# Retention and a rational feed-forward on one core: VectorE's order in the first steps of the feed-forward

## The chip, the cores and the metric

The kernel runs on one core of one Trainium2 chip. The metric is the device time of an execution in microseconds. TensorE (PE) multiplies, VectorE (DVE), ScalarE (ACT) and GpSimd (POOL) work element by element, SyncE's queue (SP) issues the transfers between HBM and the on-chip memory SBUF. Matmuls write into PSUM, a second on-chip memory that VectorE and ScalarE can read and write and GpSimd cannot.

## The reference

```python
B, H, S, D = 8, 8, 576, 64             # q, k, v: [B, H, S, D]
scores = (q @ k.T) / sqrt(D)           # per batch and head
ret = scores * gamma[h] ** (i - j)     # for i >= j, else 0; gamma[h] = 1 - 2 ** (-5 - h)
x = (ret @ v) -> [B * S, H * D]        # 4608 tokens x 512
h = x @ w_in                           # 512 -> 2048
P = a0 + a1 h + a2 h^2 + a3 h^3
Q = 1 + |b0| |h| + |b1| h^2
out = (P / (Q + 1e-6)) @ w_out         # 2048 -> 512
```

All inputs and outputs are 32-bit floats.

## The kernel before, in words

**Retention.** The tokens are cut into 36 units of 128. For a unit n, `scale_q` (GpSimd) and `scale_v` (ScalarE, eight instructions on the tile kv) scale its q and v by powers of gamma; `scores` multiplies k and q on TensorE; `decay` clears two corners of the tile s (GpSimd) and masks the scores into the rest (three VectorE instructions from PSUM). `outputs` multiplies the masked scores with v, the keys with v for the running state, and the old state with q, all into one PSUM tile ps. `add` and `fade` update the state S_sb (VectorE, then GpSimd). `keep_hi` (ScalarE) rounds the outputs to xhi, and `keep_lo` (VectorE) keeps the rest as xlo.

**Feed-forward.** The tokens are nine blocks of 512, the hidden width sixteen strips f of 128. One step works on one block and one strip (b, f). Each product is formed from high and low parts in three passes: `gemm1` is twelve matmuls into h, `gemm2` twelve into acc, three or four steps later. In between stands the rational function, spread over three steps:

- in the step of the block itself: `ffn_p` (p = a3 h + a2 and u = |h| on ScalarE, p = p h on VectorE), `ffn_p2` (VectorE, p = (p + a1) h), `ffn_va` (ScalarE, v from u), `ffn_v` (VectorE, v = v u);
- in the next: `ffn_r` (ScalarE, u = 1/Q by a logarithm and an exponential), `ffn_q` (VectorE, the quotient and one Newton factor, two instructions), `ffn_q3` (VectorE, their product);
- in the one after: `ffn_hi` (ScalarE, g high) and `ffn_lo` (g low, on GpSimd in the first 24 blocks).

h and ps lie in PSUM. u, v, p and g are in SBUF, with one exception: in steps 8 to 21 u lies in a free bank of PSUM, the tile `free_at`.

**Weights.** They arrive as raw 64-bit words (bits) and are brought into two parts in the course of the first steps: `start` (ScalarE, tile c), `split0` (VectorE, a shift of c), `split1` and `split2` (VectorE, integer operations on c and bits), `split3` (ScalarE's high part of w, then GpSimd's low part). A weight is started in one step, where `split0` follows at the end, and goes through `split1` to `split3` in the next. `STARTS` says how many are started in each step: one or two in steps 0 to 4, one in each later step.

**Order.** Each engine executes its instructions in the order in which the program writes them, and that order is written out by hand: a list of names for a step, of which `run` calls those that have something to do. So one list sets the order of VectorE, ScalarE, GpSimd, TensorE and SP at once. `BEFORE` holds for the stage ahead of the first step; `FIRST` where u is in SBUF and the step is below 24, that is in steps 0 to 7 and in 22 and 23; `MID` in steps 8 to 21; `DENSE`, `REST` and `END` after that.

```python
SCORES = [1, 3, 5, 23, 25, 27, 29, *range(2 * NF, (NB - 1) * NF, 4)]
...
        run(END if not this else MID if free_at else FIRST if i < first else DENSE if i < 2 * NF else REST, todo)
        load_weights(2)
```

In steps 1, 3, 5 and 23 a unit's scores are formed and masked; its outputs, sum, fade and x parts follow in the next step, in which the q and v of the unit after it are scaled too. Step 0 has the outputs of unit 4. Loads are issued by SP: a unit's two loads when the outputs of the unit two before it are written into the program, two weights at the end of a step as long as there are any.

Of the kernel before, what the change touches and what calls it, by code (L numbers as in the profile page):

```python
# [31 lines left out]

BEFORE = "split1 start scale_q scale_v scores decay outputs split2 add fade keep_hi keep_lo split3 split0".split()
FIRST = (
    "split1 gemm1 outputs ffn_p split2 ffn_hi keep_hi ffn_lo gemm2 ffn_r scale_q split3 add fade keep_lo start ffn_p2"
    " scale_v scores decay split0 ffn_q ffn_q3 ffn_va ffn_v"
).split()
MID = (
    "split1 split2 gemm1 ffn_p ffn_r ffn_hi ffn_lo split3 ffn_va gemm2 ffn_p2 ffn_q ffn_v ffn_q3 start split0"
# [532 lines left out]
```

## Time and profile before

| | |
|---|---|
| median of 3 runs | 962.99 us (962.88 to 964.47) |
| the profiled execution | 965.23 us, its span from first to last instruction 963.4 us |
| mean granted TensorE clock | 0.981 |
| busy: TensorE, VectorE, ScalarE, GpSimd | 922.9, 830.7, 708.9, 164.4 us |

In a row of a timeline stand the start in us from the span's start, the duration in us, the engine, the source line (L66 is the helper through which every instruction passes, so tiles tell them apart), the operation, the tiles out<-in, the sizes, and the number of equal instructions that the row merges. Brackets give idle time of the engine just ahead of the row and what ended it. An instruction's row overlaps the next one's by some 0.08 us, so the time that an instruction takes in a sequence is the distance of two starts. In the table of stages each row is a stretch of the span, with the busy time of each engine in it, the granted clock, the share of the DMA engines and their rate.

Step 0 begins at about 37 us, step 8 at about 110, step 22 at about 193 and step 24 at about 209, by VectorE's rows.

### The profile page before, as it was taken

The numbers are of one execution on the slowest core, as the hardware profiler recorded it, in microseconds if no ns is written. First come the engines' busy times: TensorE is split into PE (matmuls) and PEld (weight loads), VectorE is DVE, ScalarE is ACT, GpSimd is POOL, SyncE is SP. The second block draws the span as 40 slices with busy tenths as digits, with TensorE's granted clock in tenths as the row PEclk, the third lists the DMA queues.
The fourth block names the chain that finished last, engine by engine and source line by source line (L and its number), as shares of the span: only waits on it lengthen the run. The fifth ranks groups of instructions, "written<-read, shape, count | busy, mean of one in ns | idle before, by whom it ended". The sixth has DMA issues, their size and how long they took to land.

```text
span 963.4 us, 16126 instructions
## 1 busy us (share of the span) xinstructions
PE 922.9 (96%) x6234; PEld 750.2 (78%) x6234; DVE 830.7 (86%) x1261; ACT 708.9 (74%) x1274; POOL 164.4 (17%) x200
## 2 busy tenths in 40 slices
PE   7678889999999999999999999999999999999997
PEld 6556768877888888888888888888888888888886
DVE  3899999997889888888888888888888888888895
ACT  5477788876767778777777777777877777767775
POOL 4445444451201111010001111101111111100000
PEclk9789999999999999999999999999999999999999
DMA  9944100012221111210021112110211121001001
GB/s 347 407 183 181 39 0 1 1 45 89 88 80 53 45 45 52 80 45 25 30 80 44 44 45 88 44 67 22 88 45 45 45 88 45 1 1 45 1 0 45
DMA packets 20557, 65.44 MB, mean 68 GB/s; under 512 B 2304, under 2 KB 2432, under 8 KB 20480
## 3 DMA queue, kind: packets, MB, share of 16 engines
q1 hardware_dynamic: 20480, 64.41, 18.5%
q8 instruction: 49, 0.80, 0.4%
q14 instruction: 28, 0.23, 0.1%
HBM read 54.96 MB, written 9.44 MB: 67 GB/s over the span
## 4 chain that ended last, share of the span: by engine, by line
PE 79%; DVE 8%; ACT 6%; DMA 5%; issue 1%; POOL 1%; SPq 0%; ACTq 0%; POOLq 0%
PE acc L66 36%; PE h L66 34%; PE ps L66 8%; DMA bits<-in_w_in 3%; DVE p L66 3%; DVE c L66 2%; ACT free_at L66 2%; DVE v L66 2%; DMA bits<-in_w_out 1%; ACT v L66 1%; ACT w L66 1%; DMA qk<-in_qkv 1%; ACT g L66 1%; ACT o L66 0%; DVE s L66 0%
## 5 line engine op out<-in xcount | busy, mean ns | idle before, releaser
L66 PE MATMUL acc<-w,g 128*128 128x512 f32 x1632 | 403.7, 397 | 5.4 <-ACT o L66 5.4
L66 PE MATMUL h<-xhi,w 128*128 128x512 f32 x1152 | 381.5, 392 | 5.2 <-DVE p L66 2.7
L66 PEld LDWEIGHTS acc<-w,g 128*128 128x128 f32 x1632 | 304.9, 190 | 75.1 <-ACT o L66 6.3
L66 PEld LDWEIGHTS h<-xhi,w 128*128 128x128 f32 x1152 | 217.7, 189 | 52.6 <-DVE p L66 3.9
L66 PE MATMUL h<-xlo,w 128*128 128x512 f32 x576 | 225.6, 392 | 0.0
L66 ACT ACTIVATE p<-h,ab_sb 128x512 f32<-128x512 f32 x144 | 111.6, 775 | 108.2 <-PE h L66 108.1
L66 PEld LDWEIGHTS h<-xlo,w 128*128 128x128 f32 x576 | 108.8, 189 | 22.7 <-DVE xlo L66 0.4
L66 DVE TENSOR_TENSOR p<-p,h 128x512 f32<-128x512 f32 x144 | 98.8, 686 | 26.8 <-ACT u L66 26.3
L66 ACT ACTIVATE u<-h 128x512 f32<-128x512 f32 x130 | 77.5, 596 | 59.9 <-DVE v L66 58.3
L66 DVE SCALAR_TENSOR_TENSOR p<-p,ab_sb,u 128x512 f32<-128x512 f32 x130 | 97.8, 753 | 25.7 <-ACT u L66 22.5
L66 DVE TENSOR_TENSOR v<-v,u 128x512 f32<-128x512 f32 x130 | 91.1, 701 | 28.5 <-ACT v L66 28.4
L66 DVE SCALAR_TENSOR_TENSOR p<-p,ab_sb,h 128x512 f32<-128x512 f32 x144 | 107.2, 744 | 3.6
L66 ACT ACTIVATE v<-u,absb 128x512 f32<-128x512 f32 x130 | 104.7, 806 | 1.2 <-DVE p L66 0.9
L66 DVE SCALAR_TENSOR_TENSOR p<-v,p 128x512 f32<-128x512 f32 x144 | 100.5, 698 | 4.5
L66 ACT ACTIVATE u<-u,lnb 128x512 f32<-128x512 f32 x130 | 94.2, 724 | 4.2
L66 ACT ACTIVATE u<-v,lnb 128x512 f32<-128x512 f32 x130 | 92.8, 714 | 2.0 <-DVE v L66 2.0
L66 DVE TENSOR_TENSOR g<-p,g 128x512 fp32r<-128x512 f32 x112 | 91.4, 816 | 1.4 <-ACT g L66 1.4
L66 ACT ACTIVATE g<-p 128x512 fp32r<-128x512 f32 x136 | 85.5, 629 | 8.8 <-DVE p L66 4.2
L66 DVE SCALAR_TENSOR_TENSOR v<-v,u 128x512 f32<-128x512 f32 x130 | 90.7, 698 | 0.0
L66 POOL TENSOR_TENSOR S_sb<-S_sb,gv_sb 128x256 f32<-128x256 f32 x32 | 20.4, 637 | 403.5 <-DVE S_sb L66 401.4
L66 ACT ACTIVATE kv<-kv,gv_sb 128x64 f32<-128x64 f32 x288 | 72.6, 339 | 11.1 <-DMA kv<-in_qkv 5.6
L66 DVE TENSOR_TENSOR s<-ps,mask_sb 64x256 f32<-64x256 f32 (+1 forms) x108 | 55.0, 509 | 11.7 <-PE ps L66 10.7
(43 smaller groups left out, 696.5 us busy)
## 6 DMA issues: line engine op xcount, KB each, us to landing
qk<-in_qkv SPq DMA_DIRECT2D x36, 512.0 KB, 4.9
kv<-in_qkv SPq DMA_DIRECT2D x36, 512.0 KB, 4.0
bits<-in_w_in SPq DMA_DIRECT2D x16, 512.0 KB, 10.2
bits<-in_w_out SPq DMA_DIRECT2D x16, 512.0 KB, 10.2
out<-o SPq DMA_DIRECT2D x16, 512.0 KB, 3.5
out<-o SPq DMA_DIRECT2D x4, 256.0 KB, 2.4
gq_sb<-in_gq SPq DMA_DIRECT2D x1, 256.0 KB, 2.7
mask_sb<-in_masks SPq DMA_DIRECT2D x1, 160.0 KB, 5.1
```

Source lines behind the costliest of these rows:

```text
L66: return lambda *a, **k: self.tc.keep_in_program_order(method(*a, **k))
```

## The change

One list is rewritten. It contains the same names.

```diff
 FIRST = (
-    "split1 gemm1 outputs ffn_p split2 ffn_hi keep_hi ffn_lo gemm2 ffn_r scale_q split3 add fade keep_lo start ffn_p2"
-    " scale_v scores decay split0 ffn_q ffn_q3 ffn_va ffn_v"
+    "split1 split2 gemm1 outputs ffn_p ffn_r ffn_hi ffn_lo keep_hi split3 ffn_va gemm2 ffn_p2 add fade keep_lo"
+    " ffn_q ffn_v ffn_q3 start scale_q scale_v scores decay split0"
 ).split()
 MID = (
     "split1 split2 gemm1 ffn_p ffn_r ffn_hi ffn_lo split3 ffn_va gemm2 ffn_p2 ffn_q ffn_v ffn_q3 start split0"
```

What each engine executes in a step, in order (names stand for the instructions that the engine has of them):

| engine | before | after |
|---|---|---|
| VectorE | split1, ffn_p, split2, add, keep_lo, ffn_p2, decay, split0, ffn_q, ffn_q3, ffn_v | split1, split2, ffn_p, ffn_p2, add, keep_lo, ffn_q, ffn_v, ffn_q3, decay, split0 |
| ScalarE | ffn_p, ffn_hi, keep_hi, ffn_r, split3, start, scale_v, ffn_va | ffn_p, ffn_r, ffn_hi, keep_hi, split3, ffn_va, start, scale_v |
| GpSimd | ffn_lo, scale_q, split3, fade, decay | ffn_lo, split3, fade, scale_q, decay |
| TensorE | gemm1, outputs, gemm2, scores | the same |

## The prediction

> **What bounds the kernel now.** I read the page's busy times first, then the table of stages, then each engine's timeline in the stages that the change touches.
>
> ```profile
> PE 922.9 (96%) x6234; PEld 750.2 (78%) x6234; DVE 830.7 (86%) x1261; ACT 708.9 (74%) x1274; POOL 164.4 (17%) x200
> ```
>
> ```profile
> core 0: us, PE busy (x) PEld busy (x) DVE busy (x) ACT busy (x) POOL busy (x), PEclk, DMA share, GB/s
> 73.80:92.50 18.70, 16.20 (x128) 13.02 (x128) 18.02 (x27) 13.60 (x27) 9.80 (x9) 0.91 0.59 226
> 140.00:185.00 45.00, 45.00 (x200) 37.28 (x199) 43.82 (x71) 39.24 (x65) 19.53 (x16) 1.00 0.00 1
> 200.00:215.00 15.00, 12.88 (x95) 9.90 (x85) 14.94 (x22) 11.16 (x25) 6.53 (x7) 0.89 0.21 71
> ```
>
> Over the whole span TensorE is the bound. The table shows where it is not: in 73.8 to 92.5 (steps 4 and 5) VectorE is busy for 18.02 of 18.70 us and TensorE only 16.20; in 200 to 215 (the end of step 22, steps 23 and 24) it is 14.94 against 12.88 of 15. From 140 to 185 (the middle order) TensorE has no idle time at all. So a microsecond that VectorE gains or loses in the early steps moves the start of a stretch that TensorE fills, and reaches the end nearly whole.
>
> VectorE in steps 4 and 5, in the order of before (start, duration):
>
> ```profile
> 76.52 0.68 DVE L66 SCALAR_TENSOR_TENSOR c<-bits,c 128x512 int32<-128x512 int32 x1
> 77.12 0.68 DVE L66 TENSOR_TENSOR p<-p,h 128x512 f32<-128x512 f32 x1
> 77.72 1.17 DVE L66 SCALAR_TENSOR_TENSOR c<-bits,c 128x512 int32<-128x512 int32 x1
> 78.81 0.41 DVE L66 TENSOR_TENSOR S_sb<-S_sb,ps 128x256 f32<-128x256 f32 x1
> 79.15 0.68 DVE L66 TENSOR_TENSOR xlo<-ps,xhi 128x512 fp32r<-128x512 f32 x1
> 79.75 0.73 DVE L66 SCALAR_TENSOR_TENSOR p<-p,ab_sb,h 128x512 f32<-128x512 f32 x1
> 81.06 1.83 DVE L66 TENSOR_SCALAR c<-c 128x512 int32<-128x512 int32 x2 [0.58 <-ACT c L66]
> 82.81 0.74 DVE L66 SCALAR_TENSOR_TENSOR p<-p,ab_sb,u 128x512 f32<-128x512 f32 x1
> 84.79 0.69 DVE L66 TENSOR_TENSOR v<-v,u 128x512 f32<-128x512 f32 x1
> 85.40 2.38 DVE L66 SCALAR_TENSOR_TENSOR c<-bits,c 128x512 int32<-128x512 int32 x2
> 88.30 1.28 DVE L66 SCALAR_TENSOR_TENSOR c<-bits,c 128x512 int32<-128x512 int32 x2
> 90.17 1.55 DVE L66 TENSOR_TENSOR s<-ps,mask_sb 128x512 f32<-128x512 f32 x3
> 91.64 1.12 DVE L66 TENSOR_SCALAR c<-c 128x512 int32<-128x512 int32 x1
> 95.26 0.68 DVE L66 SCALAR_TENSOR_TENSOR c<-bits,c 128x512 int32<-128x512 int32 x1
> 116.91 0.41 DVE L66 TENSOR_SCALAR c<-c 128x512 int32<-128x512 int32 x1
> ```
>
> The two steps last from 76.52 to 95.26, 18.74 us. Equal instructions take unequal times: an integer operation 0.68 or 1.17, two of them 1.28 or 2.38, the shift 0.41 (116.91) or 1.12. GpSimd's rows of the same time, and a close-up of one meeting, say why:
>
> ```profile
> 76.80 1.55 POOL L66 TENSOR_TENSOR g<-p,g 128x512 fp32r<-128x512 f32 x1 [2.53 <-issue]
> 78.30 1.74 POOL L66 TENSOR_TENSOR qk<-qk,gq_sb 128x512 f32<-128x512 f32 x1
> 80.55 1.30 POOL L66 TENSOR_TENSOR w<-c,w 128x512 fp32r<-128x512 f32 x1 [0.51 <-ACT w L66]
> 81.81 0.79 POOL L66 TENSOR_TENSOR S_sb<-S_sb,gv_sb 128x256 f32<-128x256 f32 x1
> 85.95 1.28 POOL L66 TENSOR_TENSOR g<-p,g 128x512 fp32r<-128x512 f32 x1 [3.35 <-ACT g L66]
> 89.73 2.51 POOL L66 TENSOR_TENSOR w<-c,w 128x512 fp32r<-128x512 f32 x2 [2.49 <-ACT w L66]
> ```
>
> ```profile
> 112.26 1.28 POOL L66 TENSOR_TENSOR g<-p,g 128x512 fp32r<-128x512 f32 x1 [4.99 <-ACT g L66]
> 113.50 1.74 POOL L66 TENSOR_TENSOR w<-c,w 128x512 fp32r<-128x512 f32 x1
> 112.77 1.31 DVE L66 SCALAR_TENSOR_TENSOR p<-p,ab_sb,u 128x512 f32<-128x512 f32 x1
> 114.01 1.77 DVE L66 SCALAR_TENSOR_TENSOR v<-v,u 128x512 f32<-128x512 f32 x1
> 119.09 1.27 POOL L66 TENSOR_TENSOR g<-p,g 128x512 fp32r<-128x512 f32 x1 [3.85 <-issue]
> 120.18 0.75 DVE L66 SCALAR_TENSOR_TENSOR p<-p,ab_sb,free_at 128x512 f32<-128x512 f32 x1
> ```
>
> At 112.77 VectorE's quotient operation, all in SBUF, starts while GpSimd subtracts; it ends at 114.08, 0.54 after GpSimd's end at 113.54. GpSimd's next subtraction then takes 1.74 instead of 1.28, and VectorE's next operation 1.77 instead of 0.68: the two take turns. At 120.18 the same operation meets the same subtraction with its u in PSUM (free_at) and takes 0.75. Likewise the mask (90.17, from PSUM) takes its 1.55 beside two GpSimd subtractions. So **an SBUF-only VectorE operation that meets a GpSimd tensor operation loses up to 1.1 us (1.77 − 0.68); one on PSUM loses nothing**. Page SBUF — State Buffer of the Trainium skill, section Who interferes with whom, gives the rule: a VectorE instruction with two SBUF inputs contends with a GpSimd one that reads SBUF, whole instruction against whole instruction. The rows agree. That rule speaks against this change, which puts SBUF operations side by side.
>
> **The old pair of steps.** Collisions: 1.17 − 0.68 = 0.49 at 77.72; 1.83 − 2 x 0.41 = 1.0 at 81.06; 2.38 − 1.28 = 1.10 at 85.40; 1.12 − 0.41 = 0.71 at 91.64. Together 3.3. Waiting for ScalarE: 0.58 (81.06). The work itself is 18.74 − 3.3 − 0.58 = 14.86.
>
> **The change part by part.** No instruction and no DMA is added or removed; the list reorders VectorE, ScalarE and GpSimd. TensorE's and SP's own orders stay, so SP's loads stay in line behind the same outputs and only follow them in time; the units and weights that are loaded then are used many steps later, and I cost that at nothing. It holds in steps 0 to 7, and also in 22 and 23, which use the same list.
>
> *VectorE.* A step is now: integer operations; p x h, second p product, then (even steps) state sum and x's low part, all from PSUM; quotient, quotient, v, last product, all SBUF; (odd steps) the mask; the shifts. The PSUM run is 2 x 0.6 + 0.34 + 0.6, some 2.2 us, in an even step (start-to-start times of the rows 77.12, 78.81, 79.15 and 79.75) and 1.3 in an odd one. The SBUF run is 85.40 − 82.81 = 2.6.
>
> *GpSimd.* Scaling q goes from before the weight's subtraction to behind the state's fade. What releases its operations in an even step? ScalarE's x high part, which waits for TensorE's outputs, stands in front of ScalarE's weight copy; the fade waits for VectorE's sum; scaling q waits behind both. In the old order g and q (76.80 to 80.04) lay beside one integer operation and three PSUM operations, and cost 0.49. In the new order weight, fade and q all become ready when the PSUM run ends, and take turns with the SBUF run: 1.1 + 0.4 + 1.1 = 2.6 (the fade's 0.79 is shorter by 0.5, and loses half of itself, my choice between 0 and 0.79). The block's own g subtraction follows ScalarE's logarithm and exponential, which now stand early in its step; it meets the shift or an integer operation: 1.1, between 0 and 1.1. In an odd step g meets the third integer operation, 1.1, and of two weight subtractions one meets the quotient, 1.1 (0.6 to 2.2). Sum 5.9, bounds 3 to 7.
>
> *The mask and TensorE's outputs.*
>
> ```profile
> 73.79 2.29 PE L66 MATMUL ps<-s,kv 128*64 128x128 f32 x15 [4.59 <-POOL s L66]
> 77.83 3.02 PE L66 MATMUL acc<-w,g 128*128 128x512 f32 x12
> ```
>
> TensorE already idles 4.59 us for the masked scores (GpSimd's zeros come with them); the outputs then take 73.79 to 77.83, 4.0 us, at a low clock. In the old order VectorE has the shift, the SBUF run, two integer operations and p x h between mask and state sum: 0.4 + 2.6 + 1.2 + 0.6 = 4.8 us of work, enough for the 4.0. In the new order only the shift, two integer operations and two PSUM products lie between: 0.4 + 1.2 + 1.3 = 2.9 without collisions, 4.0 with the one of g above. So VectorE waits for outputs by 0 to 1.5; I take 0.4. The old 0.58 wait for ScalarE's integer preparation goes, since the shift stands last.
>
> New pair: 14.86 + 5.9 + 0.4 = 21.2 against 18.74, **+2.5 for steps 4 and 5** (bounds −0.5 to +4).
>
> *Other early steps.* Steps 2 and 3 are the same, but the first g there falls on PSUM work (TensorE is late with its block), one collision less: +1.4. Steps 6 and 7 have no q to scale (the next scores are in step 23): 2.5 − 1.1 = +1.4. In steps 0 and 1 q of unit 5 now waits behind two weight subtractions and the fade (2.51 + 0.79, rows 89.73 and 81.81), and the scores on TensorE wait with it; TensorE waits for that unit's mask anyway. One collision there goes, two come: +0.5. Sum for steps 0 to 7: 0.5 + 1.4 + 2.5 + 1.4 = **+5.8**.
>
> *Steps 22 and 23.*
>
> ```profile
> 201.91 1.19 DVE L66 SCALAR_TENSOR_TENSOR c<-bits,c 128x512 int32<-128x512 int32 x1
> 203.68 1.55 DVE L66 TENSOR_TENSOR s<-ps,mask_sb 128x512 f32<-128x512 f32 x3
> 205.48 1.54 PE L66 MATMUL ps<-s,kv 128*64 128x128 f32 x16 [2.08 <-POOL s L66]
> ```
>
> TensorE idles 2.08 here for the mask. The mask now stands behind the SBUF run of 2.6, in which the weight's subtraction and the next unit's q scaling meet it (1.1 for one of them), and the collision of the integer operation at 201.91 goes (1.19 − 0.68 = 0.5): **+3.2** on TensorE (bounds +1 to +4.5), which is full again behind it.
>
> **Sum.** 5.8 + 3.2 = 9.0. The profiled execution took 965.23 with a span of 963.4; the median of the runs is 962.99, 2.2 lower. 965.2 + 9.0 = 974.2 for such an execution, 963.0 + 9.0 = 972.0 for the median.
>
> A second page bears on it: TensorE: Matmul & The Clock Gate, part The HAM clock gate, says that about 3.4 us without matmuls halve TensorE's clock until as long a busy stretch has passed. The rows agree: sixteen matmuls at 205.48, behind 2.08 us, take 1.54, fifteen at 73.79, behind 4.59, take 2.29. By it the longer gap at 205 makes the outputs there slow as well: that is the last rival.
>
> **The rivals.**
> *Faster: the PSUM run covers GpSimd.* If the weight, fade and q operations end before the SBUF run starts, the pair falls to 14.86 + 0.5 for waits, 3.4 less than now; over steps 2 to 7 about 8 less, against +2.6 for the later mask in step 23: 963 − 5.5, about 957.5. It decides at whether outputs end 3 us before VectorE's low part. For it: GpSimd is busy only 9.80 of 18.70. Against: the mask's new place makes the outputs end when the PSUM run does. 13%.
> *No change, within 0.2% (1.9 us, about what a measurement of this kernel can tell from none).* Collisions only change place, 3.3 for 3.3, and the step-23 mask is hidden by the 2.08 that TensorE waits anyway: 963. Against: that wait ends with the mask itself. 6%.
> *Half of it.* Only the mask's delay in step 23 counts, or only steps 0 to 7: 963 + 3 to 5.8, 966 to 969. 18%.
> *More: TensorE's clock.* If the idle time before the outputs of steps 6 and 24 grows past what 73.79 shows, both take 4.0 instead of some 2.7 (4.0 x 1.54 / 2.29), and VectorE and ScalarE wait for them in turn: 2 x 1.3 and as much again, 3 to 6 more, 975 to 978. 15%.
> My forecast, 969 to 975: 48%.
>
> **How the numbers follow.** Faster 13%, same 6%, slower 48 + 18 + 15 = 81%. Predicted is the forecast's 972.0. The range 963 to 977.5 leaves out the faster case and the top of the last rival, under 2 in 10.
>
> **What would show it.** Right: in the new timeline the quotients and v of even steps show 1.2 to 1.8 beside weight, fade and q on GpSimd, which take turns; the pair of steps 4 and 5 takes over 20 us; TensorE's idle time for the masked scores grows in steps 2, 4, 6 and at the start of step 24 (2.08 to about 5); the stage of the middle order is as before but starts 5 to 6 us later. Wrong: the SBUF run stays at 2.6 in even steps, GpSimd's weight and q rows lie beside p x h and the low part, or TensorE's gaps shrink.

## The result, and the profile after

The changed kernel takes 974.46 us (973.88 to 974.76, 4 runs) against 963.68 (962.88 to 964.47, 4 runs): the ratio is 1.0107, with a 95% interval of 1.0093 to 1.0122. By that ratio it is slower by 10.3 us, 9.0 to 11.8. One of the ten executions of the run mixed below took 4127.63 us and is not in its ratio. The profiled execution took 974.76, its span 972.9 against 963.4.

The page's busy times, and the table of stages (steps 4 and 5 now last from 77.7 to 99.2):

```profile
PE 923.7 (95%) x6234; PEld 751.3 (77%) x6234; DVE 836.2 (86%) x1261; ACT 708.0 (73%) x1274; POOL 165.9 (17%) x200
```

```profile
77.70:99.20 21.50, 17.11 (x130) 13.86 (x131) 20.48 (x28) 13.51 (x27) 10.68 (x10) 0.82 0.42 148
150.00:195.00 45.00, 45.00 (x201) 37.24 (x200) 42.45 (x69) 38.48 (x64) 20.46 (x16) 1.00 0.00 1
210.00:225.00 15.00, 9.19 (x59) 7.19 (x59) 11.26 (x16) 5.88 (x11) 6.19 (x6) 0.77 0.22 71
```

VectorE's busy time grew by 5.5 us with the same 1261 instructions (830.7 before). The middle order is as full of TensorE work as before. In the stretch around step 24 TensorE is busy for only 9.19 of 15.00 us.

VectorE in steps 4 and 5, then GpSimd in the same time:

```profile
77.74 2.37 DVE L66 SCALAR_TENSOR_TENSOR c<-bits,c 128x512 int32<-128x512 int32 x2
82.30 0.42 DVE L66 TENSOR_TENSOR S_sb<-S_sb,ps 128x256 f32<-128x256 f32 x1 [0.82 <-ACT xhi L66]
83.24 1.47 DVE L66 SCALAR_TENSOR_TENSOR p<-p,ab_sb,u 128x512 f32<-128x512 f32 x1
84.64 1.10 DVE L66 SCALAR_TENSOR_TENSOR v<-v,u 128x512 f32<-128x512 f32 x1
85.66 1.78 DVE L66 TENSOR_TENSOR v<-v,u 128x512 f32<-128x512 f32 x1
92.42 0.93 DVE L66 SCALAR_TENSOR_TENSOR p<-p,ab_sb,u 128x512 f32<-128x512 f32 x1
93.27 1.78 DVE L66 SCALAR_TENSOR_TENSOR v<-v,u 128x512 f32<-128x512 f32 x1
94.98 1.75 DVE L66 TENSOR_TENSOR v<-v,u 128x512 f32<-128x512 f32 x1
97.25 1.55 DVE L66 TENSOR_TENSOR s<-ps,mask_sb 128x512 f32<-128x512 f32 x3
99.17 2.37 DVE L66 SCALAR_TENSOR_TENSOR c<-bits,c 128x512 int32<-128x512 int32 x2
```

```profile
82.87 1.29 POOL L66 TENSOR_TENSOR w<-c,w 128x512 fp32r<-128x512 f32 x1 [4.04 <-ACT w L66]
84.13 1.06 POOL L66 TENSOR_TENSOR S_sb<-S_sb,gv_sb 128x256 f32<-128x256 f32 x1
85.15 1.74 POOL L66 TENSOR_TENSOR qk<-qk,gq_sb 128x512 f32<-128x512 f32 x1
92.76 3.42 POOL L66 TENSOR_TENSOR w<-c,w 128x512 fp32r<-128x512 f32 x2
```

The turns are there: in step 4 weight, fade and q against quotient, quotient and v (1.47, 1.10, 1.78 where 0.7 is usual); in step 5 two weight subtractions, stretched to 3.42, against the same three. The two steps take 99.17 − 77.74 = 21.43 us, 18.74 before. TensorE's waits for the masked scores of steps 4, 6 and 24, which were 4.59, 2.46 and 2.08:

```profile
77.63 2.06 PE L66 MATMUL ps<-s,kv 128*64 128x128 f32 x16 [8.06 <-DVE s L66]
99.06 2.06 PE L66 MATMUL ps<-s,kv 128*64 128x128 f32 x16 [4.39 <-DVE s L66]
216.93 2.07 PE L66 MATMUL ps<-s,kv 128*64 128x128 f32 x16 [5.81 <-DVE s L66]
```

They are released by VectorE's mask now. Before, GpSimd's zeros ended these three waits; at step 24 they came 0.25 us after the mask (205.48 against 203.68 + 1.55). So the prediction's remark that this wait "ends with the mask itself" was not quite what its row shows. The matmuls behind the waits run at a low clock: sixteen take 2.06, and the granted clock is 0.50 from 99 to 103 us and from 216.9 to 220.

### The profile page after: what moved, and what is told of

It is laid out like the page before. It is cut to its first block, busy times and chain, and to the rows that moved or that the text cites. A ratio compares the mean times of both kernels' runs of the same rounds, so it can differ in the third digit from the quotient of the medians.

```text
span 972.9 us, 16133 instructions
## 1 busy us (share of the span) xinstructions
PE 923.7 (95%) x6234; PEld 751.3 (77%) x6234; DVE 836.2 (86%) x1261; ACT 708.0 (73%) x1274; POOL 165.9 (17%) x200
## 4 chain that ended last, share of the span: by engine, by line
PE 78%; DVE 8%; ACT 6%; issue 3%; DMA 3%; POOL 1%; SPq 0%; ACTq 0%; POOLq 0%; DVEq 0%
PE acc L66 36%; PE h L66 34%; PE ps L66 9%; DVE p L66 4%; DVE v L66 2%; ACT free_at L66 2%; DVE c L66 1%; DMA bits<-in_w_in 1%; ACT v L66 1%; DMA bits<-in_w_out 1%; DVE s L66 1%; DMA qk<-in_qkv 1%; ACT g L66 1%; ACT u L66 1%; ACT w L66 1%
## 5 line engine op out<-in xcount | busy, mean ns | idle before, releaser
L66 DVE SCALAR_TENSOR_TENSOR p<-p,ab_sb,u 128x512 f32<-128x512 f32 x130 | 101.4, 780 | 25.8 <-ACT u L66 22.5
L66 DVE TENSOR_TENSOR v<-v,u 128x512 f32<-128x512 f32 x130 | 95.4, 734 | 27.9 <-ACT v L66 27.7
L66 DVE SCALAR_TENSOR_TENSOR v<-v,u 128x512 f32<-128x512 f32 x130 | 94.2, 725 | 0.0
```

Source lines behind the costliest of these rows:

```text
L66: return lambda *a, **k: self.tc.keep_in_program_order(method(*a, **k))
```

## The experiments

Two theories. *Grouping* (the expectations also say collision theory): VectorE's SBUF operations side by side meet GpSimd's operations in turns, and that is the loss. *Mask*: the loss is the place of the mask behind that run. All ratios below are against the kernel before in runs on the same chip, with 95% intervals.

**early and late: the two places apart.**

```diff
-        ... else FIRST if i < first else ...
+        ... else FIRST if i < half else OLD if i < first else ...     # early: new list in 0 to 7
+        ... else OLD if i < half else FIRST if i < first else ...     # late: new list in 22 and 23
```

> The new list in steps 0 to 7 alone, the old one in 22 and 23. Collision theory (VectorE's SBUF-only operations meet GpSimd's reading ones in turns; the loss of each pair of steps is paid there): the lag against before at step 8 stays at 7.1 us as with the whole change, and what follows adds what the clock does at the acc wait (0 to 1.5): 6.4 to 8 us over before, 970 to 972. Rival (the late mask is the loss, and it is largest where TensorE is full right behind it, at step 24): only 3 to 5 us over before, 967 to 969.

> The old list in steps 0 to 7, the new one in 22 and 23. Prediction's term: TensorE's wait at the start of step 24 grows from 2.1 to about 5.5 us and the kernel is 3.2 us over before (+1 to +4.5): 967. If the clock at the next wait for acc decides too, as in the trace after (where 1.57 us were won back at step 28), only +1.6: 965.3. Rival (nothing of it reaches the end, as the gap is hidden later): 963.7.

Measured: early 970.53, ratio 1.0058 (1.0043 to 1.0074), 5.3 us over before; late 969.48, 1.0047 (1.0031 to 1.0064), 4.2 us. Together 9.5 of the 10.3: the parts add. Late lies in its range, 1 us above its term. Early, by its distance from before, came out between its two expectations; its 970.53 lies in the first one's range only because before took 965.24 on this chip. In the trace of early, VectorE's second product lags behind that of before by 6.3 us at step 8, by 5.5 from step 9 on, and by 3.9 from step 28 on. At step 28 twelve matmuls behind a 1.8 us wait took 3.04 in this execution and 4.61 in the profiled execution of before.

**mask: the mask ahead of the SBUF run, all else as changed.**

```diff
-    " ffn_q ffn_v ffn_q3 start scale_q scale_v scores decay split0"
+    " scores decay ffn_q ffn_v ffn_q3 start scale_q scale_v split0"
```

> The changed kernel with scores and decay ahead of ffn_q, so that VectorE's mask comes before its SBUF run; all else as changed. Collision theory: the odd steps' two weight subtractions then meet the mask (PSUM) instead of quotients and v (2.1 us less in step 5, 1.1 in step 3), VectorE's wait for the outputs in even steps goes (0.9 each), TensorE's wait at step 24 falls back by 2.6 or more; the even steps keep their 2.6 us of collisions. 9 to 10 us less than after: 964.5 to 966, not under before. Rival (the late mask is the whole loss and grouping gains by itself): under before by 2 us or more, 961.5 or less.

Measured: 965.2 against 965.24, ratio 0.9998 (0.9987 to 1.0009). The whole loss is gone, though the grouping is still there. The number lies where the collision theory had it, and so does a part of its reading: the odd run and the wait for outputs are free again, and the even run still pays turns. What it had not foreseen stands behind that. VectorE's timeline, from the two steps that took 21.43 (here from 74.57 to 91.32, 16.75) to the next state sum, and GpSimd's:

```profile
74.57 1.42 DVE L66 SCALAR_TENSOR_TENSOR c<-bits,c 128x512 int32<-128x512 int32 x2
78.22 1.01 DVE L66 SCALAR_TENSOR_TENSOR p<-p,ab_sb,u 128x512 f32<-128x512 f32 x1
86.92 1.56 DVE L66 TENSOR_TENSOR s<-ps,mask_sb 128x512 f32<-128x512 f32 x3
88.41 0.73 DVE L66 SCALAR_TENSOR_TENSOR p<-p,ab_sb,u 128x512 f32<-128x512 f32 x1
89.07 0.68 DVE L66 SCALAR_TENSOR_TENSOR v<-v,u 128x512 f32<-128x512 f32 x1
89.67 0.68 DVE L66 TENSOR_TENSOR v<-v,u 128x512 f32<-128x512 f32 x1
91.32 2.37 DVE L66 SCALAR_TENSOR_TENSOR c<-bits,c 128x512 int32<-128x512 int32 x2
97.65 0.42 DVE L66 TENSOR_TENSOR S_sb<-S_sb,ps 128x256 f32<-128x256 f32 x1 [2.58 <-ACT xhi L66]
```

```profile
86.00 1.29 POOL L66 TENSOR_TENSOR g<-p,g 128x512 fp32r<-128x512 f32 x1 [4.60 <-ACT g L66]
87.25 5.17 POOL L66 TENSOR_TENSOR w<-c,w 128x512 fp32r<-128x512 f32 x2
92.35 0.66 POOL L66 MEMSET s<- 64x256 f32 x2
```

The mask works in PSUM and lies beside the first weight subtraction again; the SBUF run of step 5 loses nothing. The 4.7 us between this pair and the changed kernel's: the odd run 2.4 (0.93, 1.78, 1.75 against 0.73, 0.68, 0.68), the first integers of step 4 0.95 (2.37 against 1.42), the quotient 0.46 (1.47 against 1.01), the wait for outputs 0.82 (82.30). The second weight subtraction paid instead: it is kept waiting until about 91.3, and the zeros of s stand behind it in GpSimd's order. TensorE's outputs of step 6 wait 3.55 us for these zeros, and VectorE's state sum waits 2.58 for the outputs. So the time level with before is a balance: steps 4 and 5 are 2.0 us shorter than before (16.75 against 18.74), and steps 6 and 7 are 5.2 longer (20.04, from 91.32 to 111.36, against 14.80).

**qfirst: GpSimd's scaling of q back in its old place, in the changed kernel.**

```diff
-    ... ffn_r ffn_hi ffn_lo keep_hi split3 ...  start scale_q scale_v scores decay split0
+    ... ffn_r ffn_hi ffn_lo scale_q keep_hi split3 ...  start scale_v scores decay split0
```

> The changed kernel with scale_q ahead of split3 on GpSimd, as it was before the change; VectorE's order as changed. Collision theory: in steps 2 and 4 q's scaling runs right behind g, over integer operations and PSUM products, and one collision of 1.1 us goes from each SBUF run, half of it coming back at the integers; step 0 gets TensorE's 3.8 us wait for q back, which VectorE does not feel: 1 to 3 us less than after, 971.5 to 973.5. Rival (the late mask is the whole loss): no change, 974.5.

Measured: 973.22, ratio 1.0095 (1.0076 to 1.0114), against 1.0107 (1.0093 to 1.0122) for the change. The intervals overlap: by the time this tells nothing. In the traces the lag at step 8 is 4.8 us instead of 7.1.

**before_w, after_w, mask_w: GpSimd's two subtractions without reading.** A memset of the same tile stands for each, in the order of before, as changed, and with the mask moved. The low parts are then zero, so these kernels leave two correction terms of the products out.

```diff
-        pool.tensor_tensor(w[:, 1, :], cf, w[:, 0, :].bitcast(F32), ALU.subtract)
+        pool.memset(w[:, 1, :].bitcast(F32), 0.0)
...
-            pool.tensor_tensor(g[:, 1, :], p, g[:, 0, :].bitcast(F32), ALU.subtract)
+            pool.memset(g[:, 1, :].bitcast(F32), 0.0)
```

> The kernel before with GpSimd's two subtractions (the low parts of the weights and of g) replaced by a memset of the same tile, which reads nothing; the low parts are zero, so this leaves two of the products' correction terms out. Collision theory: what VectorE loses to g and w (about 2.5 us of each pair of steps, 8 in all up to step 8, and 1.7 in step 8) goes: 7 to 10 us under before, 954 to 957. If the shifts (one SBUF input) still meet memsets, 1 us less of it.

> The changed kernel with the same replacement. Collision theory: the turns of g and w in the SBUF runs go (some 4 us of each pair, 13 in all), those of the fade and of q stay; what is left of the change is the later mask and two or three meetings with q: 3 to 5 us over before_w instead of 10.8. Rival (the late mask and TensorE's clock are the whole loss): as far over before_w as after is over before, 9 to 11 us.

> The kernel mask (grouped order, mask ahead of the SBUF run) with GpSimd's subtractions of the weights' and g's low parts replaced by memsets, as in before_w and after_w (two correction terms left out). Mask theory: the 9.5 us between after_w and before_w are the mask's place, so this is within 2 us of before_w, 946.5 to 950. Grouping theory (integer and PSUM operations that depend on one another side by side cost 0.1 us each, and VectorE waits otherwise): near after_w, 955 to 957.

Measured: before_w 948.06, ratio 0.9833 (0.9811 to 0.9854); after_w 957.56, 0.9935 (0.9911 to 0.9958); mask_w 947.69, 0.9828 (0.981 to 0.9847). So after_w is where the rival had it, mask_w where the mask theory had it, and before_w gained more than expected.

The two subtractions are dear: without them the kernel before is 15 us faster, where I had summed 7 to 10. This holds the meetings and whatever else a shorter GpSimd operation gives; the run does not part the two. But after_w is still 9.5 us over before_w, and the grouped order with an early mask is level with the old order (0.4 us apart, inside both intervals). With the two subtractions or without, the late mask costs the grouped order about the same: 1.0107 against 0.9998, and 0.9935 against 0.9828. So the grouping theory falls as the account of the whole loss.

The traces show that its make-up differs, though. Counted from VectorE's first integer operation of step 0 (40.46 before, where TensorE begins the step at 37; 40.63 in the changed kernel; 40.73 in before_w and 35.37 in after_w, as the stage ahead did not last equally long), after_w falls back by 3.6 us to the second product of step 8, where the changed kernel fell back by 6.9 behind before. From step 22 to step 26 it falls back by 5.2, the changed kernel by 3.4. So about half of the loss in the early steps went with the two subtractions, and more is lost at step 24. These are single executions.

What after_w waits for, in VectorE's timeline of step 4 and TensorE's at step 24, and the same place in before_w:

```profile
72.12 0.42 DVE L66 TENSOR_TENSOR S_sb<-S_sb,ps 128x256 f32<-128x256 f32 x1 [1.24 <-ACT xhi L66]
73.06 0.74 DVE L66 SCALAR_TENSOR_TENSOR p<-p,ab_sb,u 128x512 f32<-128x512 f32 x1
73.72 1.79 DVE L66 SCALAR_TENSOR_TENSOR v<-v,u 128x512 f32<-128x512 f32 x1
```

```profile
196.41 2.06 PE L66 MATMUL ps<-s,kv 128*64 128x128 f32 x16 [3.60 <-DVE s L66]
```

```profile
193.69 1.18 PE L66 MATMUL ps<-s,kv 128*64 128x128 f32 x16 [0.53 <-ACT v L66]
```

With the two subtractions out of the way, the chain itself shows: mask, outputs, x high part, state sum. In steps 4 and 5 after_w takes 2.5 us more than before_w (17.51 against 15.04): 1.24 of it is the wait for outputs, and 1.1 a turn with GpSimd's scaling of q, which still reads (73.72, 1.79 instead of 0.68).

**old_late_mask: the old list with the mask last.** Nothing grouped, one thing moved.

```diff
-    " scale_v scores decay split0 ffn_q ffn_q3 ffn_va ffn_v"
+    " scale_v split0 ffn_q ffn_q3 ffn_va ffn_v scores decay"
```

> The list of before with one thing moved: scores and decay at the end of the list, so that VectorE's mask comes last in a step (steps 0 to 7, 22 and 23); nothing is grouped. Mask theory (the place of the mask is the loss: it uncovers the two weight subtractions that lay beside it, delays the outputs and leaves TensorE idle): most of the change's 10.3 us, 7 to 10 over before. Grouping theory (SBUF operations side by side are the loss): only the delay at step 24 and some waits for outputs, 3 to 5 over before.

Measured: 982.41, ratio 1.0187 (1.0168 to 1.0207), 19 us over before, far past both expectations, and 8 over the change itself. The state sum follows close behind the mask in the old list (three operations, against five in the new one), and waits in VectorE's timeline; beside it TensorE's:

```profile
79.26 1.55 DVE L66 TENSOR_TENSOR s<-ps,mask_sb 128x512 f32<-128x512 f32 x3
81.94 1.16 DVE L66 SCALAR_TENSOR_TENSOR c<-bits,c 128x512 int32<-128x512 int32 x1
85.75 0.42 DVE L66 TENSOR_TENSOR S_sb<-S_sb,ps 128x256 f32<-128x256 f32 x1 [2.65 <-ACT xhi L66]
```

```profile
81.07 2.07 PE L66 MATMUL ps<-s,kv 128*64 128x128 f32 x16 [9.26 <-DVE s L66]
```

The mask's place alone costs more than the whole change. In the trace 12.7 us of it are there at step 8. The grouped order has a late mask too and costs 8 us less; it pushes the state sum back behind both products, where the wait for outputs is 0.82 instead of 2.65.

**clear, mixed and clear_q: towards a better list.** From the trace of mask: write the zeros of s ahead of the weight's subtraction. `clear(n)` holds the two memsets of `decay`.

```diff
-    "... ffn_r ffn_hi ffn_lo keep_hi split3 ..."
+    "... ffn_r ffn_hi ffn_lo clear keep_hi split3 ..."            # clear, on top of mask
+    "... ffn_r ffn_hi ffn_lo scale_q clear keep_hi split3 ..."    # clear_q: and q's scaling too
-        ... else FIRST if i < first else ...
+        ... else OLD if i in (6, 7) else FIRST if i < first else ...   # mixed, on top of clear
```

> The kernel mask (changed order with the mask ahead of the SBUF run) with the zeros of s written by GpSimd ahead of the weight's subtraction instead of behind it. In the trace of mask a weight subtraction of step 5 was kept waiting from 88.5 to 91.3 while VectorE ran five SBUF operations, and outputs(7) waited for the zeros behind it: TensorE idled 3.5 us more than the mask asked for. If that is the cost, outputs(7) start 3 us or more earlier: 2.5 to 4 us less than mask, 961 to 962.5 where mask has 965. Rival (outputs do not bound VectorE there, and it is taken back by collisions): as mask, 965.

> The kernel clear with the old list in steps 6 and 7, where grouping cost most (18.0 us against 14.8 for the two steps in the trace after). Collision theory: the lead that mask has over before at step 6 (4.2 us) is kept to step 8 and 0.5 to 1 more is won in step 22: 4 to 6 us under before, 959 to 961. Rival (what is won early is lost again before step 8 whatever the list): as clear.

> The kernel clear with scale_q ahead of the weight's subtraction on GpSimd. Collision theory: in steps 2 and 4 q's scaling then runs beside second product, state sum and low part, and one turn of 1.1 us with v goes in each; in step 0 TensorE's wait of 3.8 us for the scaled q goes, which brought a low clock and a late outputs(5): 1.5 to 3 us less than clear, 956.5 to 958. Rival (the weight's subtraction takes the place that q leaves in the SBUF run): as clear, 959.5.

Measured: clear 959.4, ratio 0.9957 (0.9943 to 0.9971), below mask's interval; mixed 963.34, 0.999 (0.9975 to 1.0006), slower than clear, against my expectation; clear_q 958.89, 0.9948 (0.9933 to 0.9963), not to be told from clear. From the first integer operation of step 4 to the outputs of step 6 pass 14.5 us in clear and 18.1 in mask, so the earlier zeros did what was expected of them. Steps 6 and 7 take 13.53 us in clear, and 14.80 in mixed as in before: with outputs in time the grouped list is the faster one there, and that grouping cost most in these steps was wrong. This is 1.3 of the 3.9 us between mixed and clear; the rest no trace shows, as the profiled execution of mixed (961.23) was faster than that of clear (962.49). TensorE's wait for the masked scores of step 6 in clear_q:

```profile
88.39 1.07 PE L66 MATMUL ps<-s,kv 128*64 128x128 f32 x15 [0.52 <-DVE s L66]
```

It is 0.52 us (2.46 before, 3.55 in mask), and fifteen matmuls behind it take 1.07, where fifteen took 1.51 before and 2.12 in mask. Clear and clear_q beat the kernel before, by 4.0 and 4.4 us. How much of this earlier zeros would give in the old list, where zeros ended TensorE's waits too, no run shows.

## Why the prediction was right, and where its reasons were not

The size and the sign held: 972.0 forecast, 974.46 measured, in the range. Of the signs named, the quotients and v of step 4 show 1.47, 1.10 and 1.78, the pair of steps 4 and 5 takes 21.43, and TensorE's waits in steps 4, 6 and 24 grew. At step 2 the wait shrank, from 3.40 to 0.23, because TensorE had already waited 3.79 for the scaled q of that unit. The middle stage begins 7.1 us later, not 5 to 6. By terms, from the lag behind before, up to step 8 of the first integer operation of each pair of steps and from there of the second product:

| term | predicted | in the traces |
|---|---|---|
| steps 0 and 1 | +0.5 | −0.1 (step 0 began 0.2 late) |
| steps 2 and 3 | +1.4 | +1.3 |
| steps 4 and 5 | +2.5 | +2.7 |
| steps 6 and 7 | +1.4 | +3.2 |
| steps 8 to 21 | 0 | −0.7, then +1.5 at a wait for acc |
| steps 22 to 24 | +3.2 | +3.1 |
| step 28 | 0 | −1.6 |
| sum | +9.0 | +9.4 |

The sum came out better than its terms, and that is luck: steps 6 and 7 cost 1.8 more than forecast and steps 0 and 1 0.6 less, 0.7 came back just behind step 8, and the two clock effects nearly cancel. The term for steps 22 to 24 is two errors that cancel. The SBUF run of step 23 met GpSimd twice (211.18 and 213.45) and took 4.8 us, where I had 2.6 and one turn of 1.1; and step 22, which I had not counted, became 1.0 shorter.

```profile
211.18 1.75 DVE L66 SCALAR_TENSOR_TENSOR v<-v,u 128x512 f32<-128x512 f32 x1
213.45 1.75 DVE L66 SCALAR_TENSOR_TENSOR p<-v,p 128x512 f32<-128x512 f32 x1
215.12 1.55 DVE L66 TENSOR_TENSOR s<-ps,mask_sb 128x512 f32<-128x512 f32 x3
```

- *Collisions.* The rule that an SBUF operation loses up to 1.1 us and a PSUM one nothing held in the rows shown, and the new pair's sum was 5.9 against some 5.6 in the rows. That q's move would cost a turn with v in step 4 is in the row at 85.66.
- *The step that failed is what the collisions were charged to.* I charged them to the SBUF operations standing side by side, and the mask's place with 3.2 us at step 24 and 0.4 a pair. The runs mask and mask_w show that the grouped order as a whole costs nothing by time when the mask stands ahead of the SBUF run (0.9998; 0.9828 against 0.9833). The even run keeps its turns even so (1.8 us in step 4 of mask); they are outweighed by what the old list lost. The late mask costs in three ways: the two weight subtractions beside which it stood meet the SBUF run instead (2.4 us in step 5), VectorE waits for outputs, and TensorE waits at step 24. I had quoted the mask beside two such subtractions at no cost, and did not ask what they would meet when it left; in the sum the turn is there, but not its cause.
- *The wait for outputs* I took as 0.4; it is 0.82 in the rows of steps 4 and 5, and 1.24 or 2.65 where collisions do not hide it. It and the collisions do not simply add: where the collisions are fewer, as in after_w, the wait is longer.
- *Steps 6 and 7* were got by taking one turn from the pair before. Counted by themselves they have no mask and no second weight, and before loses less there than in the pair before; outputs at a low clock come on top (next point). Measured are 14.80 us before and 18.00 after.
- *The clock* (last rival) did go low behind the waits of 4.39 and 5.81 us, as section The HAM clock gate of the Trainium skill's page TensorE: Matmul & The Clock Gate has it. At step 6 the outputs took 3.9 instead of 2.6 us, the 1.3 of the rival. At step 24 nothing was lost: outputs and the twelve matmuls behind them took 5.9 together, and 6.5 before, where those twelve had run at a low clock. So the 3 to 6 us did not come. The clock also gave +1.5 and −1.6 at waits of 3.6 and 1.8 that are in both kernels. The second is shorter than the idle window of some 3.4 us that this section of the Trainium skill gives, yet behind it the kernel before ran at a granted clock of 0.62 and the changed one at 1.00; and behind 3.63 early took 3.01 for the twelve matmuls that took 4.34 before and 5.49 after the change. In these rows the length of the wait alone does not decide it.

## What to carry to other kernels

Before moving an operation, list what runs beside it on other engines: an operation that costs and loses nothing there (here the mask from PSUM) is cover, and moving it exposes whatever it covered. Where an element-wise step feeds TensorE and its result comes back to the same engine, keep that step early and its consumer late; the distance between them in work is the slack. Test a reason by doing the suspected part alone in the old kernel and undoing it alone in the new one: a right sum does not show its cause, as here. And look into the trace even where the time is as expected: a level time can be a gain and a loss.

## What the runs showed of the hardware that I had not expected

VectorE and GpSimd do not always take turns. In mask, at 88.41, VectorE's run began without having waited, and five SBUF operations passed at their usual times while GpSimd's second subtraction, which with its neighbour took 5.17 us instead of 2.5, stood until that run was over, at about 91.3. In the changed kernel, at 92.42, the run began with a wait (0.93), and from there each side went once. What decides this is not settled. GpSimd's memsets, which only write, cost VectorE's SBUF operations nothing that can be seen. From after_w, VectorE's timeline and GpSimd's:

```profile
81.09 0.75 DVE L66 SCALAR_TENSOR_TENSOR p<-p,ab_sb,u 128x512 f32<-128x512 f32 x1
```

```profile
81.09 0.53 POOL L66 MEMSET g<- 128x512 f32 x1
```

The quotient takes its usual 0.75 in the very time of the memset of g, as section Who interferes with whom of the Trainium skill's page SBUF — State Buffer has it for instructions that only write; in the kernel before the same two operations as subtractions made 15 us of difference, of which the share of the meetings is not measured.
